# Moving the sums of inputs for the block products behind units of the second pass's first chunk

## Chip, cores and metric

One core of a Trainium2 chip runs the kernel. The metric is the device time of one execution in microseconds (us); lower is better. Several executions are timed and their median is given, and one more is recorded by the profiler.

## What is computed

Attention over 4 batches and 12 heads (448 positions, 64 wide) gives x of 1792 x 768. Two feed-forward layers follow, each with 2048 hidden columns:

```python
def _moe_ref(x, w_in, w_out, s, b):
    h = x @ w_in
    r = np.maximum(h, 0.0)
    g = s * (r * r) + b
    return g @ w_out

def _moe2_ref(x, w_in, w_out):
    h = x @ w_in
    g = h * np.cos(h)
    return g @ w_out

def reference(q, k, v, g_q, g_k, moe, moe2):
    x = attention(q, k, v, g_q, g_k).transpose(0, 2, 1, 3).reshape(1792, 768)
    return _moe2_ref(_moe_ref(x, **moe), **moe2)
```

All of it is fp32. The change touches the first layer alone, and in it only the input product `x @ w_in` of batches 2 and 3.

## The kernel before

**Products.** TensorE takes fp32 operands as two parts, a high one (a cast, made on ScalarE) and a low one (value minus high, a subtraction on VectorE or GpSimd). Each product is three matmuls: high by high, high by low, low by high. Weights are tiles wh, wl; inputs xha, xla; hidden values gh, gl. A matmul here has 128 rows of contraction, 128 rows out and 448 columns, one batch.

**Staging.** The hidden columns are cut into 8 chunks of two 128-row blocks. The list `segs` sets the order: segments 0 to 2 do layer 1 for batches 0 and 1 beside the attention, segment 3 does layer 1 for batches 2 and 3 (the second pass), segment 4 is layer 2. A chunk has input units (`unit_in`: 18 matmuls into a PSUM tile ph, then ScalarE's relu r, GpSimd's square r2, VectorE's scale and bias gt, ScalarE's cast gh and GpSimd's low part gl) and 12 output units per pair of batches (`unit_out_1`: 6 matmuls into a PSUM tile po, which on the first visit ScalarE copies to acc and later VectorE adds to acc).

**The second pass.** Its first chunk is done with four plain input units (two blocks for batch 2, then two for batch 3: 72 matmuls) and its 12 output units, the six of batch 2 ahead of the six of batch 3 (72 matmuls). From the second chunk on, `unit_seven` replaces the four input units of a chunk by seven block products of 9 matmuls (a11, s2, s3, s1, a12, a22, s4). They need sums of the weight blocks (`load_combined`: tiles rs, ts, cast to wsh and low part wsl) and sums of the input blocks t1 to t4. The input sums are made once, by `combine_x(c)` for c = 0, 1, 2: four DMAs bring blocks from DRAM into tiles xc, VectorE makes four differences in place (lines 624 to 627), ScalarE four casts into xhb (line 630), VectorE two and GpSimd two low parts into xlb (line 631). `unit_seven` sums its products in two tiles uh and ul (line 683 on VectorE, line 700 the copy of the first product on ScalarE), with one buffer each. Its PSUM tiles share three buffers of tag ph with `unit_in`; po has three buffers too.

**Where the pools meet.** At `("next", 3)` the attention's pools are closed and the pools xb, mb and psb are opened. The PSUM banks of psb were those of other tiles until then, and the first ph of the second pass has to wait for the last adds to acc of the segment before. The tiles xc share one ring of 8 buffers (tag "acc" in mb) with the weight sums wsh and wsl of `load_combined`: xc of c = 2 takes the places of c = 0, and the weight sums of chunk 1 take the places of c = 1.

**Order.** The program runs under a scheduling context that decides the order of instructions on each engine; each engine then runs its own list in order. Two helpers bind it: `follow` adds a real wait, `issue_after` only an order. The dictionary `marks` holds instructions that later ones are put behind.

The call before the change, in the main loop over units:

```python
                pools["psb"] = ctx.enter_context(tc.tile_pool(name="psb", bufs=2, space=PSUM))
                for c in range(NE // 2):
                    combine_x(c)
            continue
```

Of the kernel before, what the change touches and what calls it, by code (L numbers as in the profile page):

```python
# [10 lines left out]
F32 = mybir.dt.float32  # L11
# [4 lines left out]
ALU = mybir.AluOpType  # L16
# [27 lines left out]
def body(ctx, tc, q, k, v, g_q, g_k, w1_in, w1_out, s_in, b_in, w2_in, w2_out, out):  # L44
    nc = tc.nc
    B, H, S, D = q.shape
    E = out.shape[1]
    F = w1_in.shape[1]
    P = 128
# [6 lines left out]
    NE = E // P  # L56
# [5 lines left out]
    NT = 2 * S // P  # L62
# [19 lines left out]
    pools = {"att": att_scope.enter_context(tc.tile_pool(name="att", bufs=2))}  # L82
# [6 lines left out]
    sb = const.tile([P, 2], F32, tag="sb", name="sb")  # L89
# [10 lines left out]
    marks = {}  # L100
# [5 lines left out]
    def issue_after(later, earlier):  # L106
        info = mybir.DependencyInfo(mybir.DependencyClass.NoSync, mybir.DependencyReason.DATA)
        tc.add_manual_dep(later.ins, earlier.ins.name, info, reason="issue order")
# [9 lines left out]
    def home(layer, b):  # L118
        return held_x["b" if layer and b < 2 else "a"]
# [10 lines left out]
    def wide(layer, seg, ck):  # L130
        return layer == 1 or seg == 3 and 0 < ck < NCK - 1

    def span(layer, seg, ck, b):
        cut = WIDE if wide(layer, seg, ck) else S
        return slice(cut, 2 * S) if b % 2 else slice(0, cut)

    def products(w, x):
        return ((w[0], x[0]), (w[1], x[0]), (w[0], x[1]))
# [478 lines left out]

    mixed = {}

    def combine_x(c):  # L620
        x11, x12, x21, x22 = (pools["mb"].tile([P, E], F32, tag="acc", name=f"xc_{c}_{n}", bufs=2 * NT - NE)[:, :S] for n in range(4))
        for t, b, cc in ((x11, 2, c), (x12, 3, c), (x22, 3, c + NE // 2), (x21, 2, c + NE // 2)):
            nc.sync.dma_start(t, stash[0, b, cc])
        nc.vector.tensor_tensor(x11, x12, x11, ALU.subtract)
        nc.vector.tensor_tensor(x12, x22, x12, ALU.subtract)
        nc.vector.tensor_tensor(x22, x22, x11, ALU.subtract)
        nc.vector.tensor_tensor(x21, x21, x22, ALU.subtract)
        for n, (name, t) in enumerate((("t1", x11), ("t3", x12), ("t2", x22), ("t4", x21))):
            hi, lo = mixed[name, c] = [z[:, n // 2 * S:(n // 2 + 1) * S] for z in held_x["b"][c + n % 2 * (NE // 2)]]
            nc.scalar.copy(hi, t)  # L630
            (nc.vector if n % 2 else nc.gpsimd).tensor_tensor(lo, t, hi.bitcast(F32), ALU.subtract)  # L631

    g = {}
    acc = {}
# [3 lines left out]
    def g_pair(key, seg):  # L638
        n = count["pairs"] % (5 if seg > 3 else 4)
        count["pairs"] += 1  # L640
        if "mb" not in pools or n < 3:
            gp, tag, nb = ma, "g", 3
        else:
            gp, tag, nb = pools["mb"], "gx"[n - 3], 1
        return [gp.tile([P, 2 * S], F32R, tag=tag + z, name=f"g{z}_{key}", bufs=nb) for z in "hl"]

    def squared(h, key, place=None):
        def temp(pool, tag, name):
            return pool.tile([P, WIDE], F32, tag=tag, name=f"{name}_{key}")[:, :h.shape[1]]

        r = temp(ma, "t0", "r") if place is None else place
        nc.scalar.activation(r, h, AF.Relu)
        r2 = temp(pools["mb"], "t1", "r2") if "mb" in pools else r
        nc.gpsimd.tensor_tensor(r2, r, r, ALU.mult)
        gt = temp(ma, "t2", "gt")
        nc.vector.tensor_scalar(gt, r2, sb[:, 0:1], sb[:, 1:2], ALU.mult, ALU.add)
        return gt

    def unit_seven(layer, seg, ck, *_):
# [55 lines left out]
    def unit_in(layer, seg, ck, f, b):  # L715
        ft = ck * CF + f
        key = f"{layer}_{ft}_{b}"
        wh, wl = weights[layer, seg, 0, ft, 0]
        wh, wl = (z.rearrange("p (c f) -> p c f", f=P) for z in (wh, wl))
        pool, tag, bufs = (pools["psb"], "ph", 3) if "psb" in pools else (psm, "mo", 2)  # L720
        ph = pool.tile([P, 512], F32, tag=tag, name=f"ph_{key}", bufs=bufs)
        at = span(layer, seg, ck, b)
        size = at.stop - at.start
        h = ph[:, :size]

        def temp(pool, tag, name):
            return pool.tile([P, WIDE], F32, tag=tag, name=f"{name}_{key}")[:, :size]

        for c in range(NE):
            x = [z[:, at] for z in home(layer, b)[c]]  # L730
            for n, (a, m) in enumerate(products((wh[:, c, :], wl[:, c, :]), x)):
                nc.tensor.matmul(h, a, m, start=(c == 0 and n == 0), stop=(c == NE - 1 and n == 2))  # L732
            if c % 2 and c < NE - 1:
                yield 1.13
        if count["g"] % 2 == 0:
            pair[:] = g_pair(key, seg)
        to = at if wide(layer, seg, ck) else slice(count["g"] % 2 * S, (count["g"] % 2 + 1) * S)
        gh, gl = (z[:, to] for z in pair)
        count["g"] += 1
        if layer == 0:  # L740
            gt = squared(h, key)
        else:
            hs = temp(ma, "t0", "hs")
            marks["hs"] = nc.scalar.copy(hs, h)
            h = hs
            kk = temp(pools["mb"], "t1", "kk")
            nc.scalar.activation(kk, h, AF.Copy, scale=1.0 / (2 * math.pi), bias=MAGIC)
            nc.scalar.activation(kk, kk, AF.Copy, bias=-MAGIC)  # L748
            gt = temp(ma, "t2", "gt")
            nc.vector.scalar_tensor_tensor(gt, kk, -C1, h, ALU.mult, ALU.add)  # L750
            nc.vector.scalar_tensor_tensor(gt, kk, -C2, gt, ALU.mult, ALU.add)
            nc.scalar.activation(gt, gt, AF.Abs)
            nc.scalar.activation(gt, gt, AF.Sin, scale=-1.0, bias=halfpi)  # L753
            nc.gpsimd.tensor_tensor(gt, h, gt, ALU.mult)  # L754
        nc.scalar.copy(gh, gt)  # L755
        nc.gpsimd.tensor_tensor(gl, gt, gh.bitcast(F32), ALU.subtract)  # L756
        g[ft, b] = (gh, gl)
        if layer == 1 and b % 2:
            g[ft, "pair", b // 2] = list(pair)
        yield 1.13  # L760
# [173 lines left out]
    def ahead(n):  # L934
        while todo and todo[0][0] - AHEAD * (todo[0][1][0] == "s") <= n:
            count["needed"], key = todo.pop(0)
            if key[0] == "s":
                load_combined(key[1])
            else:
                load_weight(key)  # L940
# [3 lines left out]
    def until(batches):  # L944
        while finished["pairs"] < batches * NP:
            next(steps)
# [9 lines left out]
    debt = 0.0  # L956
    seg = 0
    soon, again = [], []
    wait = 0
    for n, u in enumerate(units):  # L960
        count["unit"] = n
        ahead(n + LOOK)
        if u[0] == "next":
            seg = u[1]
            if seg == 1:
                until(2)
            if seg == 3:
                for _ in steps:
                    pass
                att_scope.close()  # L970
                pools["xb"] = ctx.enter_context(tc.tile_pool(name="xb", bufs=1))
                held_x["b"] = paired(pools["xb"], "b")
                pools["mb"] = ctx.enter_context(tc.tile_pool(name="mb", bufs=2))
                pools["psb"] = ctx.enter_context(tc.tile_pool(name="psb", bufs=2, space=PSUM))
                for c in range(NE // 2):
                    combine_x(c)
            continue
        if wait:
            wait -= 1
        elif soon:  # L980
            reload(*soon.pop(0))
        elif again:
            reload(*again.pop(0))
        if u[0] == "in":
            while soon and len(xs.get((u[1], u[5]), [])) < NE:
                reload(*soon.pop(0))
            while again and u[1] == 1:
                reload(*again.pop(0))
        for cost in {"in": unit_in, "seven": unit_seven, "out": unit_out}[u[0]](*u[1:]):
            debt += cost * rates[min(seg, 1)]  # L990
            while debt > 0:
                c = next(steps, None)
                if c is None:
                    break
                debt -= c
        if u[0] == "seven" and u[3] == NCK - 1:
            again = [(1, b, c) for b in range(2) for c in range(NE)]
        if n in last:
            until(last[n] + 1)
            if finished["pairs"] == B * NP:  # L1000
                fetch(last[n])
                wait = 3
            soon += [(0, last[n], c) for c in range(NP)]
# [28 lines left out]
```

## Time and profile before

| | |
|---|---|
| median of 3 executions | 1250.6 us (1248.45 to 1252.15) |
| the profiled execution | 1251.13 us, span 1249.3 us |
| busy share of the span | PE 98%, PE weight loads 83%, DVE 72%, ACT 62%, POOL 52% |
| mean granted TensorE clock | 0.996 |
| chain that ended last | PE 79%, DVE 4%, POOL 2%, DMA 2%, ACT 2% |
| longest waits of PE | 6.6 us (one, first ph of the second pass), 4.0 us in 3, 2.9 us in 2 |

PE is TensorE, PEld its weight loads, DVE is VectorE, ACT ScalarE, POOL GpSimd, SP SyncE (it issues the DMAs). Times in rows are microseconds from the start of the span unless they say ns. A bracket behind a row of a timeline gives the idle time of the engine just before it and what ended that. Since PE is busy for 98% of the span, time on the other engines counts where PE waits for them.

### The profile page before, as it was taken

Reading aid. Unit: us, or ns where it says so; the run is one execution under the profiler, and the core shown is the slowest. Engines: PE = TensorE matmul, PEld = TensorE weight load, DVE = VectorE, ACT = ScalarE, POOL = GpSimd, SP = SyncE. Lnnn points to the kernel's source line nnn. Section 1 sums busy time; section 2 is a strip of 40 time slices with the busy share of each in tenths; the row PEclk is TensorE's granted clock in tenths of the full one; section 3 lists DMA queues with packets and bytes.
Section 4 is the critical chain, followed back from the end, with each engine's and each line's share of the span. In section 5 each row is a group of like instructions: output and inputs, shape, how many; then the busy total and the mean of one; then the engine's idle time right before and its main releaser. Section 6 shows DMA issues by size and latency. Waiting matters only on the chain.

```text
span 1249.3 us, 18909 instructions
## 1 busy us (share of the span) xinstructions
PE 1219.8 (98%) x6566; PEld 1033.2 (83%) x6566; DVE 894.0 (72%) x1514; ACT 768.8 (62%) x1705; POOL 648.7 (52%) x758
## 2 busy tenths in 40 slices
PE   7999999999999999979999999999999999999998
PEld 5555777778777877978899889899999999999997
DVE  6888778777768764785877788575777766676765
ACT  4788888776657653545334346698666766565640
POOL 4777647464544534765554544556454535353541
PEclk9999999999999999989999999999999999999999
DMA  4334336334333433451222241131111111111105
GB/s 120 98 104 121 105 99 193 113 131 141 107 123 97 128 112 122 159 176 46 76 58 64 72 144 43 35 109 57 51 51 51 51 51 51 51 51 52 55 9 177
DMA packets 88462, 114.07 MB, mean 91 GB/s; under 512 B 11952, under 2 KB 78512, under 8 KB 88368
## 3 DMA queue, kind: packets, MB, share of 16 engines
q1 hardware_dynamic: 88048, 112.66, 29.6%
q8 instruction: 51, 0.84, 0.3%
q14 instruction: 43, 0.35, 0.1%
q10 hardware_dynamic: 320, 0.23, 0.1%
HBM read 89.26 MB, written 23.59 MB: 90 GB/s over the span
## 4 chain that ended last, share of the span: by engine, by line
PE 79%; DVE 4%; POOL 2%; DMA 2%; ACT 2%; issue 1%; SPq 0%; DVEq 0%; ACTq 0%; POOLq 0%
PE ph L732 27%; PE po L810 18%; PE po L784 15%; PE av L406 4%; PE tp L371 4%; PE sc L319 4%; PE ph_s L676 3%; PE ph_a L676 2%; DMA t<-wd 1%; POOL xlb L631 1%; DVE wl L537 1%; PE rt L390 1%; DMA rs<-wd 0%; PE pt_q L276 0%; POOL wsl L603 0%
## 5 line engine op out<-in xcount | busy, mean ns | idle before, releaser
L537 POOL TENSOR_TENSOR wl<-t,wh 128x384 fp32r<-128x384 f32 x128 | 140.5, 1114 | 88.6 <-ACT wh L534 82.0
L756 POOL TENSOR_TENSOR gl<-gt,gh 128x512 fp32r<-128x512 f32 (+1 forms) x100 | 120.2, 1213 | 114.7 <-ACT gh L755 114.5
L732 PE MATMUL ph<-xha,wh 128*128 128x448 f32 (+2 forms) x408 | 152.1, 373 | 6.8 <-DVE acc L792 6.6
L810 PE MATMUL po<-wh,gh 128*128 128x384 f32 x448 | 152.0, 340 | 1.3 <-DVE acc L818 1.3
L818 DVE TENSOR_TENSOR acc<-po,acc 128x384 f32<-128x384 f32 x196 | 105.3, 551 | 64.2 <-PE po L810 63.9
L732 PE MATMUL ph<-xha,wl 128*128 128x448 f32 (+2 forms) x408 | 150.3, 368 | 0.0
L810 PE MATMUL po<-wh,gl 128*128 128x384 f32 x448 | 150.1, 335 | 0.0
L810 PE MATMUL po<-wl,gh 128*128 128x384 f32 x448 | 149.5, 335 | 0.0
L732 PE MATMUL ph<-xla,wh 128*128 128x448 f32 (+2 forms) x408 | 149.5, 368 | 0.0
L754 POOL TENSOR_TENSOR gt<-hs,gt 128x512 f32<-128x512 f32 x64 | 76.7, 1205 | 117.1 <-ACT gt L753 113.3
L792 DVE TENSOR_TENSOR acc<-po,acc 128x448 f32<-128x448 f32 (+2 forms) x168 | 101.5, 617 | 45.2 <-PE po L784 44.4
L578 DVE SCALAR_TENSOR_TENSOR t<-c,t 128x384 uint32<-128x384 uint32 x128 | 97.6, 765 | 40.2 <-ACT t L572 36.8
L534 ACT CAST wh<-t 128x384 fp32r<-128x384 f32 x172 | 82.5, 511 | 62.6 <-PE po L784 20.0
L346 ACT ACTIVATE pr<-sc,top 128x448 f32<-128x448 f32 x161 | 102.2, 640 | 17.2 <-DVE top L334 16.6
L334 DVE TENSOR_REDUCE top<-sc 128x1 f32<-128x448 f32 x168 | 98.2, 615 | 16.2 <-PE sc L319 15.4
L571 ACT ACTIVATE c<-raw 128x384 f32<-128x384 f32 x128 | 71.2, 558 | 52.4 <-DVE t L579 16.4
L371 PE MATMUL tp<-ident,pr 128*112 128x128 f32 x672 | 94.9, 278 | 1.6 <-ACT pT L385 0.7
L371 PEld LDWEIGHTS tp<-ident,pr 128*112 128x112 f32 x672 | 74.5, 134 | 25.5 <-issue 13.3
L732 PEld LDWEIGHTS ph<-xha,wh 128*128 128x128 f32 x408 | 77.3, 189 | 17.4 <-ACT xhb L630 6.9
L810 PEld LDWEIGHTS po<-wh,gh 128*128 128x128 f32 x448 | 84.0, 188 | 8.9 <-DVE acc L818 6.1
L579 DVE SCALAR_TENSOR_TENSOR t<-c,t 128x384 uint32<-128x384 uint32 x128 | 88.3, 693 | 1.8
L750 DVE SCALAR_TENSOR_TENSOR gt<-kk,hs 128x512 f32<-128x512 f32 x64 | 55.5, 869 | 47.2 <-ACT kk L748 26.6
(182 smaller groups left out, 3232.5 us busy)
## 6 DMA issues: line engine op xcount, KB each, us to landing
raw<-in_moe_w_in_dram SPq DMA_DIRECT2D x64, 384.0 KB, 3.5
raw<-in_moe_w_out_dram SPq DMA_DIRECT2D x64, 384.0 KB, 3.2
wd<-t SPq DMA_DIRECT2D x64, 192.0 KB, 2.6
t<-wd SPq DMA_DIRECT2D x44, 192.0 KB, 2.4
rawk<-in_k_dram SPq DMA_DIRECT2D x24, 224.0 KB, 2.8
rawv<-in_v_dram SPq DMA_DIRECT2D x24, 224.0 KB, 3.0
rs<-wd SPq DMA_DIRECT2D x28, 192.0 KB, 2.6
rawq<-in_q_dram SPq DMA_DIRECT2D x23, 192.0 KB, 2.8
```

The lines of the kernel that those rows point to most:

```text
L334: line("DVE", nc.vector.tensor_reduce(top, st[i]["sc", c][j][1][:, :S], axis=AX.X, op=ALU.max, negate=True))
L346: e = line("ACT", nc.scalar.activation(pr, sc[:, :S], AF.Exp, bias=st[i]["top"][:, at], scale=scale, accum_out=st[i]["sums"][:, at]))
L371: mm = [nc.tensor.transpose(tp[:, kc * P:(kc + 1) * P], pr[:, kc * CP:(kc + 1) * CP], ident) for kc in range(NCH)]
L537: casts.append((count["needed"], z, eng, eng.tensor_tensor(wl, w, wh.bitcast(F32), ALU.subtract)))
L578: nc.vector.scalar_tensor_tensor(t, c, 0x80000000, t, ALU.bitwise_and, ALU.bitwise_or)
L579: nc.vector.scalar_tensor_tensor(t, c, 3, t, ALU.logical_shift_left, ALU.bitwise_or)
L732: nc.tensor.matmul(h, a, m, start=(c == 0 and n == 0), stop=(c == NE - 1 and n == 2))
L756: nc.gpsimd.tensor_tensor(gl, gt, gh.bitcast(F32), ALU.subtract)
L784: marks["out"] = nc.tensor.matmul(po, a, m, start=(f == 0 and n == 0), stop=(f == CF - 1 and n == 2))
L792: nc.vector.tensor_tensor(at, po, at, ALU.add)
L810: nc.tensor.matmul(po, a, m, start=(f == 0 and n == 0), stop=(f == CF - 1 and n == 2))
L818: nc.vector.tensor_tensor(at, po, at, ALU.add)
```

## The change

`combine_x` is cut in two: `fetch_x(c)` issues the four DMAs, `combine_x(c)` the arithmetic. At `("next", 3)` only `fetch_x(0)` and `fetch_x(1)` are called. The arithmetic is called in the loop over units, behind the third, fourth and sixth place after it: c = 0 behind the second input unit, c = 1 behind the third, c = 2 behind the first output unit; `fetch_x(2)` stands directly behind `combine_x(0)`. The first difference of each c is put behind the latest gt on VectorE, and each cast xhb behind the latest gh on ScalarE. No instruction is added or taken away; every engine has as many rows as before. Lines from 624 on stand 3 lines lower after the change (624 is 627, 631 is 634, 656 is 659, 732 is 735), those from 756 on in `unit_out_1` as well (790 is 793, 792 is 795).

```diff
-    def combine_x(c):
-        x11, x12, x21, x22 = (pools["mb"].tile([P, E], F32, tag="acc", name=f"xc_{c}_{n}", bufs=2 * NT - NE)[:, :S] for n in range(4))
+    def fetch_x(c):
+        x11, x12, x21, x22 = mixed["raw", c] = [pools["mb"].tile([P, E], F32, tag="acc", name=f"xc_{c}_{n}", bufs=2 * NT - NE)[:, :S] for n in range(4)]
         for t, b, cc in ((x11, 2, c), (x12, 3, c), (x22, 3, c + NE // 2), (x21, 2, c + NE // 2)):
             nc.sync.dma_start(t, stash[0, b, cc])
-        nc.vector.tensor_tensor(x11, x12, x11, ALU.subtract)
+
+    def combine_x(c):
+        x11, x12, x21, x22 = mixed.pop(("raw", c))
+        issue_after(nc.vector.tensor_tensor(x11, x12, x11, ALU.subtract), marks["gt"])
...
-            nc.scalar.copy(hi, t)
+            issue_after(nc.scalar.copy(hi, t), marks["gh"])
...
-        nc.vector.tensor_scalar(gt, r2, sb[:, 0:1], sb[:, 1:2], ALU.mult, ALU.add)
+        marks["gt"] = nc.vector.tensor_scalar(gt, r2, sb[:, 0:1], sb[:, 1:2], ALU.mult, ALU.add)
...
-        nc.scalar.copy(gh, gt)
+        marks["gh"] = nc.scalar.copy(gh, gt)
...
-                for c in range(NE // 2):
-                    combine_x(c)
+                for c in range(2):
+                    fetch_x(c)
+                sums = {n + 2: (0,), n + 3: (1,), n + 5: (2,)}
...
+        for c in sums.get(n, ()):
+            combine_x(c)
+            if c == 0:
+                fetch_x(2)
```

**First place: VectorE, the last adds to acc of the segment before, ahead of the second pass's first matmul.** The adds are those of line 792 (795 after); wl_3_0_1_0 is the low part of the second block of the first chunk's weights. Before:

```order
L624 TENSOR_TENSOR xc_0_6679<-xc_1_6680,xc_0_6679 128x448
L631 TENSOR_TENSOR xlb_6648<-xc_1_6660,xhb_6647 128x448
L537 TENSOR_TENSOR wl_3_0_1_0_6543<-t_3_0_1_0_0_6544,wh_3_0_1_0_6542 128x384
L627 TENSOR_TENSOR xc_2_6661<-xc_2_6661,xc_3_6662 128x448
L792 TENSOR_TENSOR acc_0_3_0_2425<-po_0_3_1_6596,acc_0_3_0_2425 128x448
L537 TENSOR_TENSOR wl_3_0_1_0_6543<-t_3_0_1_0_1_6548,wh_3_0_1_0_6542 128x384
L625 TENSOR_TENSOR xc_1_6680<-xc_3_6682,xc_1_6680 128x448
L792 TENSOR_TENSOR acc_0_4_0_2482<-po_0_4_1_6606,acc_0_4_0_2482 128x448
L792 TENSOR_TENSOR acc_0_5_0_2519<-po_0_5_1_6616,acc_0_5_0_2519 128x448
```

After:

```order
L537 TENSOR_TENSOR wl_3_0_1_0_6543<-t_3_0_1_0_0_6544,wh_3_0_1_0_6542 128x384
L795 TENSOR_TENSOR acc_0_3_0_2425<-po_0_3_1_6596,acc_0_3_0_2425 128x448
L537 TENSOR_TENSOR wl_3_0_1_0_6543<-t_3_0_1_0_1_6548,wh_3_0_1_0_6542 128x384
L795 TENSOR_TENSOR acc_0_4_0_2482<-po_0_4_1_6606,acc_0_4_0_2482 128x448
L795 TENSOR_TENSOR acc_0_5_0_2519<-po_0_5_1_6616,acc_0_5_0_2519 128x448
```

The differences xc and the low part xlb are gone from between the adds; the two halves of wl_3_0_1_0 still stand ahead of the last two adds.

**Second place: VectorE, from the end of the first chunk's input units to the first weight sum of chunk 1.** wsl_0 is the low part of the product a11's weights. Before, with no gt of batch 2 or 3 ahead of these rows:

```order
L631 TENSOR_TENSOR xlb_6648<-xc_2_6661,xhb_6647 128x448
L626 TENSOR_TENSOR xc_3_6682<-xc_3_6682,xc_0_6679 128x448
L631 TENSOR_TENSOR xlb_6650<-xc_1_6680,xhb_6649 128x448
L624 TENSOR_TENSOR xc_0_6699<-xc_1_6700,xc_0_6699 128x448
L537 TENSOR_TENSOR wl_3_1_0_0_6587<-t_3_1_0_0_1_6592,wh_3_1_0_0_6586 128x384
L627 TENSOR_TENSOR xc_2_6681<-xc_2_6681,xc_3_6682 128x448
```

After:

```order
L659 TENSOR_SCALAR gt_1_3_6885<-r_0_1_3_6883,sb 128x448
L627 TENSOR_TENSOR xc_0_6743<-xc_1_6744,xc_0_6743 128x448
L628 TENSOR_TENSOR xc_1_6668<-xc_3_6670,xc_1_6668 128x448
L628 TENSOR_TENSOR xc_1_6744<-xc_3_6746,xc_1_6744 128x448
L629 TENSOR_TENSOR xc_3_6670<-xc_3_6670,xc_0_6667 128x448
L629 TENSOR_TENSOR xc_3_6746<-xc_3_6746,xc_0_6743 128x448
L630 TENSOR_TENSOR xc_2_6669<-xc_2_6669,xc_3_6670 128x448
L634 TENSOR_TENSOR xlb_6650<-xc_1_6668,xhb_6649 128x448
L630 TENSOR_TENSOR xc_2_6745<-xc_2_6745,xc_3_6746 128x448
L634 TENSOR_TENSOR xlb_6652<-xc_1_6744,xhb_6651 128x448
L603 TENSOR_TENSOR wsl_0_6761<-rs_0_6751,wsh_0_6760 128x384
```

The sums of c = 1 and c = 2 now stand behind the last gt of the first chunk (gt_1_3) and ahead of the weight sum that chunk 1's first product needs.

**Third place: GpSimd, the same stretch.** gl_0_3 are the low parts of the hidden values of batch 3, xlb_6644 and xlb_6646 the sums' low parts. Before:

```order
L631 TENSOR_TENSOR xlb_6644<-xc_0_6679,xhb_6643 128x448
L631 TENSOR_TENSOR xlb_6644<-xc_3_6682,xhb_6643 128x448
L631 TENSOR_TENSOR xlb_6646<-xc_0_6699,xhb_6645 128x448
L654 TENSOR_TENSOR r_0_0_2_6742<-r_0_2_6740 128x448
L603 TENSOR_TENSOR wsl_1_6787<-ts_0_6781,wsh_1_6786 128x384
```

After:

```order
L657 TENSOR_TENSOR r_0_1_3_6883<-r_1_3_6881 128x448
L759 TENSOR_TENSOR gl_0_3_6806<-gt_0_3_6811,gh_0_3_6805 128x448
L634 TENSOR_TENSOR xlb_6644<-xc_0_6667,xhb_6643 128x448
L759 TENSOR_TENSOR gl_0_3_6806<-gt_1_3_6885,gh_0_3_6805 128x448
L634 TENSOR_TENSOR xlb_6646<-xc_0_6743,xhb_6645 128x448
L634 TENSOR_TENSOR xlb_6644<-xc_3_6670,xhb_6643 128x448
L603 TENSOR_TENSOR wsl_0_6761<-ts_1_6758,wsh_0_6760 128x384
```

The low parts xlb stood ahead of the first square r of batch 2; they now stand behind the last square of batch 3, mixed with the low parts gl that the output units read.

## Rows read from the trace of the kernel before

**Rows 1.** Page: busy time of each engine and share of the span.

```profile
PE 1219.8 (98%) x6566; PEld 1033.2 (83%) x6566; DVE 894.0 (72%) x1514; ACT 768.8 (62%) x1705; POOL 648.7 (52%) x758
```

**Rows 2.** Waits of PE: line and releaser; us in total, times, longest.

```profile
PE ph L732 <- DVE acc L792: 6.6, 1, 6.6
```

**Rows 3.** PE timeline, early and around the first ph: start, us, operation, idle before.

```profile
16.21 1.63 PE L319 MATMUL sc<-kT,qT 64*128 64x448 f32 x4 [2.87 <-ACT pr L346]
...
536.80 0.37 PE L784 MATMUL po<-gl,wh 128*128 128x448 f32 x1
543.75 0.71 PE L732 MATMUL ph<-xha,wh 128*128 128x448 f32 x1 [6.58 <-DVE acc L792]
...
545.00 0.57 PE L732 MATMUL ph<-xha,wh 128*128 128x448 f32 x1
545.38 0.57 PE L732 MATMUL ph<-xha,wl 128*128 128x448 f32 x1
...
549.45 0.37 PE L732 MATMUL ph<-xha,wl 128*128 128x448 f32 x1
549.66 0.36 PE L732 MATMUL ph<-xla,wh 128*128 128x448 f32 x1
```

**Rows 4.** DVE timeline, 541 to 551.

```profile
541.04 0.95 DVE L537 TENSOR_TENSOR wl<-t,wh 128x384 fp32r<-128x384 f32 x1
...
542.46 1.14 DVE L792 TENSOR_TENSOR acc<-po,acc 128x448 f32<-128x448 f32 x2
...
550.15 0.61 DVE L631 TENSOR_TENSOR xlb<-xc,xhb 128x448 fp32r<-128x448 f32 x1
550.69 0.61 DVE L627 TENSOR_TENSOR xc<-xc,xc 128x448 f32<-128x448 f32 x1
```

**Rows 5.** ACT timeline, 537 to 553.

```profile
537.89 0.51 ACT L534 CAST wh<-t 128x384 fp32r<-128x384 f32 x1 [1.78 <-DMA t<-wd]
...
547.25 0.57 ACT L630 CAST xhb<-xc 128x448 fp32r<-128x448 f32 x1 [0.44 <-DVE xc L627]
...
552.77 0.54 ACT L652 ACTIVATE r<-ph 128x448 f32<-128x448 f32 x1
```

**Rows 6.** Windows: stretch, length, busy PE, PEld, DVE, ACT, POOL, then PEclk, DMA share, GB/s.

```profile
17.00:18.00 1.00, 1.00 (x5) 0.23 (x2) 0.40 (x2) 0.82 (x4) 0.26 (x1) 0.50 0.64 199
...
544.00:546.00 2.00, 2.00 (x6) 1.78 (x7) 2.00 (x5) 0.83 (x2) 0.19 (x1) 0.50 0.98 323
```

**Rows 7.** POOL timeline, 545 to 559 and 586 to 595.

```profile
545.81 7.62 POOL L631 TENSOR_TENSOR xlb<-xc,xhb 128x448 fp32r<-128x448 f32 x2 [4.23 <-ACT xhb L630]
...
555.26 1.30 POOL L631 TENSOR_TENSOR xlb<-xc,xhb 128x448 fp32r<-128x448 f32 x1
556.53 1.33 POOL L603 TENSOR_TENSOR wsl<-rs,wsh 128x384 fp32r<-128x384 f32 x1
557.82 1.47 POOL L756 TENSOR_TENSOR gl<-gt,gh 128x448 fp32r<-128x448 f32 x1
...
586.38 1.16 POOL L695 TENSOR_TENSOR gl_s<-gt_s,gh_s 128x448 fp32r<-128x448 f32 x1 [2.53 <-ACT gh_s L694]
...
593.65 1.08 POOL L654 TENSOR_TENSOR r_s<-uh 128x448 f32<-128x448 f32 x1
```

**Rows 8.** DVE timeline, 555 to 560.

```profile
555.48 2.80 DVE L603 TENSOR_TENSOR wsl<-rs,wsh 128x384 fp32r<-128x384 f32 x2
558.19 1.57 DVE L631 TENSOR_TENSOR xlb<-xc,xhb 128x448 fp32r<-128x448 f32 x1
```

**Rows 9.** ACT timeline, where chunk 2's first product is copied.

```profile
594.76 0.53 ACT L700 COPY uh<-ph_a 128x448 f32<-128x448 f32 x1 [0.22 <-POOL r_s L654]
```

**Rows 10.** PE timeline, 553 to 600: the rows with idle before them.

```profile
577.55 0.47 PE L784 MATMUL po<-gh,wh 128*128 128x448 f32 x1 [0.57 <-ACT acc L790]
...
595.35 0.47 PE L676 MATMUL ph_s<-xhb,wsh 128*128 128x448 f32 x1 [0.23 <-ACT uh L700]
...
598.07 0.51 PE L784 MATMUL po<-gh_s,wh 128*128 128x512 f32 x1 [0.63 <-ACT gh_s L694]
```

More of the change, by code (lines that the diff above doesn't have):

```diff
@@ L958, in body @@
     soon, again = [], []
+    sums = {}
     wait = 0
```

## The prediction, made before the changed kernel was run

> **What bounds the kernel now.** The page comes first: TensorE is busy for 98% of the span [rows 1], so an edit on the other engines counts only where TensorE waits, or where its clock is low. The list of its waits shows where: one wait of 6.6 us stands out, the first ph of the second pass behind the last adds to acc [rows 2]. The timeline of TensorE shows it: the last po begins at 536.80, the first ph at 543.75 after 6.58 us of idle [rows 3]. Behind the gap the matmuls come 0.375 us apart, later 0.203 [rows 3]. [...] From 543.75 to the end of the wide spacing at 548.7 there are some 14 matmuls, each late by 0.17, so the low clock costs 2.4 us. The timelines of VectorE and ScalarE say what the gap is made of: differences of xc stand between the adds, the last two adds run at 542.46 [rows 4], and a half of a weight cast waits for its DMA until 537.89 [rows 5].
>
> **Term 1, the gap closes in part.** The cast at 537.89 and its DMA [rows 5] stay where they are: on SP nothing ahead of that DMA moves, and the four DMAs of c = 2 only go further back. In the new order VectorE's wl of that cast still stands ahead of the last two adds. So: cast done at 538.4, wl 0.55, two adds 1.14 [rows 4], and 0.15 to the matmul as now (543.60 to 543.75), which is 540.2. TensorE idles 3.0 us instead of 6.58: **-3.6**. The bounds are 0 (if something else were to hold the bank) and -4.1 (if the wl were free earlier); the chain above is made of rows only, so I take its value.
>
> **Term 2, the clock.** The nearest row to a 3.0 us gap is the one of 2.87 us at 16.21, and there the clock fell as well, to 0.50 [rows 3, 6]; but TensorE was only partly busy before it, while here it comes from full work. So the clock may stay up at this gap (-2.4) or not (0). The terms below give two more gaps of about 3 us, each of which can bring it down. I count one low stretch, as now: **0**, with -2.4 and +2.4 (two stretches) kept as ends.
>
> **Term 3, the sums now fall into the first chunk's own work.** What hid them was the gap and the 72 matmuls of the input units, in which GpSimd had little else to do. From 540.2, the 72 matmuls take 14.6 us (0.203 each [rows 3]), to 554.8; the 42 output matmuls of batch 2 and of the first of batch 3 would end at 563.3, and then the first product of chunk 1 wants its weight sum. Behind the last ph come r (0.54 [rows 5]), its square (1.0) and gt (0.5), at 557.0. Then VectorE has ten operations up to that weight sum, 0.54 each [rows 4], 5.3 us, and GpSimd five (two gl, three xlb; one xlb pair also holds the ring places that the weight sum needs), 1.14 each as in undisturbed rows [rows 7], 5.7 us. If the two run side by side the weight sum's cast and low part (1.0) end at 563.7: 0.4 us of wait. If they exclude one another it is 557.0 + 11.0 + 1.0 = 569.0: 5.7 us. The rows speak for exclusion: two xlb on GpSimd, 2.3 us of work, took 7.62 us while VectorE ran differences and low parts back to back up to 551.3 [rows 4, 7]; and from 555.26 to 559.76 three operations of GpSimd and three of VectorE, 4.8 us of work by their undisturbed durations, took 4.5 us [rows 7, 8]. So I take 5.7, and 0.9 more because the sums and their casts are handed between VectorE and ScalarE (two waits of 0.44 in the trace, one of them in [rows 5]), now with copies of po between them on ScalarE: **+6.6**, between 0.4 and 9. It will show in pieces: at the later po of batch 2, whose three banks wait for ScalarE's copies, at the first po of batch 3 (low part gl on GpSimd), and at ph of product a11.
>
> [...]
>
> **Term 4, chunk 1 runs without cover.** Before, output matmuls of the first chunk stood between the products of chunk 1. Now most are spent earlier, and s1, a12, a22, s4 and chunk 2's a11, s2, s3 follow one another directly. Chunk 2's s1 is the fourth user of three PSUM banks and needs the copy of a11 into uh, which waits for the last square r_s of chunk 1 [rows 9]. From the end of chunk 1's s1, TensorE has six products to do, 54 x 0.203 = 11.0 us. GpSimd has seven operations up to that square, 1.05 each in the rows, 7.4 us, with 1.8 ahead (add and relu) and 0.6 behind (the copy): 9.8, no wait. With operations stretched by VectorE as at 555.26 to 557.82 (1.3 to 1.47 instead of about 1.1 [rows 7]) it is 12 to 13, a wait of 1 to 2; with the four waits for casts that these seven rows had before, the longest 2.53 and 4.6 in all [rows 7], a wait of 3.4 to 4.6. I take **+3.3**, with 0 and 6 as ends, since the casts and gt still stand in the same rows.
>
> **Term 5.** The three small waits of the trace at 577.55, 595.35 and 598.07 lie in the stretch that is now ordered otherwise [rows 10]; terms 3 and 4 take their place: **-1.4**.
>
> **Sum.** -3.6 + 0 + 6.6 + 3.3 - 1.4 = **+4.9**. Beyond 600 TensorE has next to no idle time, so the shift stays to the end. The sum is made against the profiled execution, 1251.1, which stands 0.5 above the median; against the median it is 1250.6 + 4.9 = **1255.5**.
>
> **Rivals.**
> - *The forecast*, both port-bound waits appear and the clock has one low stretch: 1253 to 1258. Chance 0.45.
> - *The sums slip in between (the other side).* If GpSimd's five operations and VectorE's ten overlap by more than about two thirds, term 3 is 2 or less and term 4 is 0 to 1: -3.6 + 1.5 + 0.5 - 1.4 = -3.0 with a low stretch, -5.4 without one: 1245 to 1248. For it: GpSimd has no run of more than five such operations, and VectorE's timeline has gaps in which they could go. Against it: the two overlaps above. Chance 0.15.
> - *Gain and loss cancel.* Term 3 about 4, term 4 about 1.5, clock up: -3.6 - 2.4 + 4 + 1.5 - 1.4 = -1.9; with the low stretch +0.5: 1248.5 to 1252. For it: these terms are bounded by 0.4 and 0 below. Chance 0.25.
> - *The clock falls twice*, at the first gap and at one of the later ones: +2.4, 1258 to 1260. Chance 0.10.
> - *The change doesn't do what it says*, because the first ph waits for something other than the adds: term 1 is 0, the rest as above or less, 1254 to 1259. The releaser named is the add, which speaks against it. Chance 0.05.
>
> **How the numbers follow.** About 0.3%, 3.75 us, is what can be told from no change. Faster than 1246.85 is two thirds of the second case and a little of the third: 0.13. Within: the rest of the second, nearly all of the third, a third of the forecast: 0.40. Slower than 1254.35: two thirds of the forecast and the last two cases: 0.47. The range from 1247 to 1259.5 leaves out about a tenth below and less above. The likeliest sign's own range is 1253 to 1258.
>
> **What would show it right or wrong.** The wait of the first ph falls to about 3.0 us and its matmul starts near 540.2 (right), or stays over 5 (term 1 wrong). New waits of PE between 558 and 572, on ScalarE's copies of po, on gl and on the weight sum, 6 to 7 us in all; GpSimd's xlb and gl of several us beside VectorE's run (term 3). One wait of 3 us or more of a product of chunk 2 on the copy into uh (term 4). The windows' granted clock at the gaps (term 2). If the new waits add up to under 4 us, the forecast falls and the kernel is level or faster.

## The result: slower by 0.8%, as forecast in sign and twice as much in size

The changed kernel takes 1259.86 us (median of 4, 1258.54 to 1261.97), the kernel before 1250.46 beside it: a ratio of 1.0077, 95% interval 1.0056 to 1.0098. The forecast was 1255.5, with a range up to 1259.5. So the sign was right, the size was not: +9.4 us where +4.9 was forecast, and the measured time lies just above the range.

The page of the changed kernel, its span, its engines (compare [rows 1]) and the clock in 40 slices:

```profile
span 1260.2 us, 18915 instructions
...
PE 1224.3 (97%) x6566; PEld 1035.3 (82%) x6566; DVE 902.2 (72%) x1514; ACT 769.7 (61%) x1705; POOL 647.2 (51%) x758
...
PEclk9999999999999999998999999999999999999999
```

The same line of the clock before:

```profile
PEclk9999999999999999989999999999999999999999
```

TensorE does the same matmuls and is busy for 4.5 us longer, and the mean granted clock of the profiled execution has fallen from 0.996 to 0.991. That is the first hint that idle time is not the whole loss. The slices are too coarse to show it: one slice stands below 9 in both kernels. The waits of TensorE from 530 to 640, which answer to [rows 2] (line and releaser; us in total, times, longest):

```profile
PE ph_s L679 <- ACT uh L703: 4.1, 1, 4.1
PE ph_a L679 <- DVE wsl L603: 3.3, 1, 3.3
PE ph L735 <- DVE acc L795: 3.3, 1, 3.3
```

The one wait of 6.6 us is now 3.3, and new ones of its size follow; two smaller groups are left out here. The timeline of TensorE shows where; it answers to [rows 3] and [rows 10]:

```profile
536.96 0.37 PE L787 MATMUL po<-gl,wh 128*128 128x448 f32 x1
540.61 0.44 PE L735 MATMUL ph<-xha,wh 128*128 128x448 f32 x1 [3.28 <-DVE acc L795]
...
563.54 0.47 PE L787 MATMUL po<-gh,wh 128*128 128x448 f32 x1 [1.67 <-ACT acc L793]
565.43 0.74 PE L787 MATMUL po<-gh,wh 128*128 128x448 f32 x1 [0.41 <-ACT acc L793]
568.41 0.74 PE L787 MATMUL po<-gh,wh 128*128 128x448 f32 x1 [0.36 <-ACT acc L793]
574.70 0.48 PE L679 MATMUL ph_a<-xha,wsl 128*128 128x448 f32 x1 [3.31 <-DVE wsl L603]
600.17 0.44 PE L679 MATMUL ph_s<-xhb,wsh 128*128 128x448 f32 x1 [1.33 <-ACT gh_s L697]
606.33 0.74 PE L679 MATMUL ph_s<-xhb,wsh 128*128 128x448 f32 x1 [4.06 <-ACT uh L703]
```

And the windows show the clock there (stretch, length, busy us of PE, PEld, DVE, ACT, POOL, then granted clock, DMA share, GB/s; compare [rows 6]):

```profile
542.00:544.00 2.00, 2.00 (x7) 1.74 (x6) 1.28 (x3) 0.51 (x1) 0.00 (x0) 0.50 0.90 314
...
566.00:568.00 2.00, 2.00 (x6) 1.30 (x4) 2.00 (x2) 1.07 (x3) 2.00 (x2) 0.50 0.00 0
...
576.00:578.00 2.00, 2.00 (x6) 1.76 (x6) 1.33 (x1) 0.49 (x2) 0.85 (x1) 0.50 0.00 0
...
607.00:609.00 2.00, 2.00 (x7) 1.78 (x6) 1.50 (x3) 0.56 (x1) 1.07 (x2) 0.50 0.35 100
```

Four stretches at a granted clock of 0.50 instead of 1.00, 541 to 544.7, 565 to 572, 575.4 to 578.8 and 606 to 609.5, where the kernel before has one.

**The account closes.** A late row marks the whole shift, the first input product of layer 2 that waits for ScalarE. Before and after:

```profile
798.71 0.44 PE L732 MATMUL ph<-xha,wh 128*128 128x384 f32 x1 [0.27 <-ACT hs L744]
809.56 0.44 PE L735 MATMUL ph<-xha,wh 128*128 128x384 f32 x1 [0.27 <-ACT hs L747]
```

With the 0.16 us that separated the runs already at 536.8 taken off, the shift is 10.7 us. Idle time of TensorE between the two marks: before 6.58 + 0.57 + 0.23 + 0.63 and one of 0.92 at 612.1, together 8.9; after the seven above and one of 0.24 at 762.6, together 14.7. That is +5.7. Clock: TensorE is busy at a granted clock of 0.50 for 5.2 us before and some 15.6 us after; matmuls come 0.375 us apart there instead of 0.203, so 0.46 of each such us is lost, 2.4 before and 7.2 after. That is +4.8. Together 10.5 of 10.7. (The profiled execution is the slowest of the four; the median shifts by 9.4.)

### The profile page after: what moved, and what is told of

Same layout as the page of the kernel before. It is cut to its first block, busy times and chain, and to the rows that moved or that the text cites. A ratio compares the mean times of both kernels' runs of the same rounds, so it can differ in the third digit from the quotient of the medians.

```text
span 1260.2 us, 18915 instructions
## 1 busy us (share of the span) xinstructions
PE 1224.3 (97%) x6566; PEld 1035.3 (82%) x6566; DVE 902.2 (72%) x1514; ACT 769.7 (61%) x1705; POOL 647.2 (51%) x758
## 4 chain that ended last, share of the span: by engine, by line
PE 80%; DVE 5%; issue 1%; POOL 1%; DMA 1%; ACT 1%; SPq 0%; DVEq 0%; ACTq 0%; POOLq 0%
PE ph L735 27%; PE po L813 18%; PE po L787 16%; PE av L406 4%; PE tp L371 4%; PE sc L319 4%; PE ph_s L679 3%; PE ph_a L679 2%; DMA t<-wd 1%; PE rt L390 1%; DVE wl L537 1%; PE pt_q L276 0%; DVE acc L795 0%; PE pt_k L276 0%; POOL wl L537 0%
## 5 line engine op out<-in xcount | busy, mean ns | idle before, releaser
L334 DVE TENSOR_REDUCE top<-sc 128x1 f32<-128x448 f32 x168 | 98.2, 615 | 16.4 <-PE sc L319 15.6
```

Source lines behind the costliest of these rows:

```text
L334: line("DVE", nc.vector.tensor_reduce(top, st[i]["sc", c][j][1][:, :S], axis=AX.X, op=ALU.max, negate=True))
```

## The experiments

Theory: the sums, put behind the first chunk's units, hold up GpSimd and VectorE, which take turns there (one operation of each per 1.53 us), and through them TensorE; behind the waits of 3.28, 3.31 and 4.06 us the granted clock was 0.50 as well. Rivals: the ring of tiles or the later DMAs; each engine's own queue; a clock that only takes the place of waiting.

**1. The split without the order.**

```diff
-        issue_after(nc.vector.tensor_tensor(x11, x12, x11, ALU.subtract), marks["gt"])
+        nc.vector.tensor_tensor(x11, x12, x11, ALU.subtract)
...
-            issue_after(nc.scalar.copy(hi, t), marks["gh"])
+            nc.scalar.copy(hi, t)
```

> The changed kernel without its two order marks: the DMAs are still issued apart and the sums are still called in the loop, but nothing binds them behind gt or gh. The scheduler then puts the differences back between the adds to acc, as before. Theory (the new place of the sums on VectorE and GpSimd makes all of the loss): the first ph waits 6.6 us again, one low stretch of the clock, no wait on a weight sum or on uh over 1 us, 1250.5 within 2. Rival (the later DMAs of c = 2 and the shared ring make part of the loss): 1253 or more, with waits on DMAs of xc or on ring places.

Measured: 1251.72, ratio 1.0006 (0.9997 to 1.0015), the first ph waits 7.5 us again, no other wait over 1 us. The split of the DMAs costs nothing that can be told; the scheduler puts the sums back into the gap. All of the loss comes from the order on VectorE. (The mark on ScalarE's casts adds nothing to it: without that mark alone the program has the same instructions in the same order on every engine as the changed kernel.)

**2. Sums behind the adds only.**

```diff
-        nc.vector.tensor_tensor(at, po, at, ALU.add)
+        marks["add"] = nc.vector.tensor_tensor(at, po, at, ALU.add)
...
-        nc.vector.tensor_tensor(x11, x12, x11, ALU.subtract)
+        issue_after(nc.vector.tensor_tensor(x11, x12, x11, ALU.subtract), marks["add"])
```

> The kernel before, with one edit: the first difference of each c is put behind the last add to acc, so the sums leave the gap but run in the stretch of the 72 input matmuls and not behind it. Theory (closing the gap alone is worth about 3.3 us, and the sums cost what they hold up on GpSimd): first ph waits 3.0 to 3.3, then waits of 3 to 7 us in all at the output matmuls of batch 2, because GpSimd's squares and low parts gl stand behind the sums; 1248 to 1254. Rival (the sums have free cover under the 72 matmuls): 1246 or less with no wait over 1 us behind the first.

Measured: 1249.93, ratio 0.9998 (0.9988 to 1.0007). Its waits of TensorE:

```profile
PE ph_s L676 <- ACT wsh L602: 3.6, 1, 3.6
PE ph L732 <- DVE acc L792: 3.1, 1, 3.1
```

The gap closes as far as in the changed kernel, and 3.6 us come back, though not where I expected them: not at the output matmuls, but at chunk 1's second product, behind the weight sum. TensorE idles less than before up to layer 2 (7.5 us against 8.9), but the granted clock falls to 0.50 twice, at 540 and at 567 (mean of the profiled execution 0.995, before 0.996). Closing the gap is worth about what the displaced work then costs. What loses time is therefore not that the sums left the gap, but how far they went.

**3. Low parts on VectorE.**

```diff
-            (nc.vector if n % 2 else nc.gpsimd).tensor_tensor(lo, t, hi.bitcast(F32), ALU.subtract)
+            nc.vector.tensor_tensor(lo, t, hi.bitcast(F32), ALU.subtract)
```

> The changed kernel with all twelve low parts xlb on VectorE (0.54 us each there, 1.14 on GpSimd), none on GpSimd. Theory (VectorE's two-input operations and GpSimd's exclude one another, so their sum counts): the sum of work in the stretch falls by some 3 us, the waits of term 3 from 5.75 to 2 to 4, the wait on uh stays at 4 or more; 1257 to 1259. Rival (each engine's own queue is the bound): VectorE, with more to do, comes later to the weight sum, the waits grow by 1.5 or more; 1261 or more.

Measured: 1256.22, ratio 1.0046 (1.0031 to 1.0061). VectorE has six operations more, and TensorE waits 11.6 us from 530 to 640 instead of 14.4. Its three longest groups:

```profile
PE ph_s L679 <- ACT uh L703: 5.9, 1, 5.9
PE ph L735 <- DVE acc L795: 2.9, 1, 2.9
PE po L787 <- ACT acc L793: 1.5, 2, 0.8
```

The wait of 3.3 us on the weight sum is gone; the rest of term 3 is 1.5 us, less than the 2 to 4 expected, and the time is a little under the range given. The rival is out: a longer queue on VectorE made the weight sum come sooner. The trace of this run shows why: GpSimd has nothing to do from 564.5 to 566.7, and VectorE's operations there come 0.54 us apart, against 1.5 in the changed kernel. The wait on uh has grown from 4.1 to 5.9 us, and two of the four low stretches of the clock are gone: matmuls come 0.37 us apart from 540.9 to 543.2 and from 600.5 to 604.7, but 0.20 from 567.8 to 580.5.

**4. Fillers in the waits.** 50 matmuls whose results nobody reads, in the four places where TensorE waited:

```diff
+    def filler(n, behind):
+        pt = psm.tile([P, 512], F32, tag="mo", name=f"fill_{count['fill']}", bufs=2)[:, :S]
+        count["fill"] += 1
+        x = home(0, 2)[0][0]
+        for k in range(n):
+            z = nc.tensor.matmul(pt, x[:, :P], x[:, :S], start=True, stop=True)
...
+            if (ck, wn) == (1, "a11"):
+                last[:] = [filler(13, outs_of[0, 0, 3])]
+            if (ck, wn) == (2, "s1"):
+                last[:] = [filler(17, last[0])]
```

> The changed kernel with 50 more matmuls of 448 columns on TensorE (10.2 us at 0.203 each), whose results nobody reads, put into the four places where it waited: 13 ahead of the first ph, 7 ahead of the fifth po of batch 2, 13 ahead of product a11 of chunk 1, 17 ahead of product s1 of chunk 2. Nothing else waits for them. Theory (four stretches at the lower clock cost some 7 us, against 2.4 in the kernel before): the engine is busy through the waits, the granted clock stays at 1.00 behind them, the first product of each place starts when it did or up to 1 us later, and the time falls by 4 to 7 us, to 1253 to 1256. Rival (the low clock only takes the place of waiting for other engines): the time stays within 1.5 us of 1259.9 or grows by what the fillers overrun.

Measured: 1256.55, ratio 1.0047 (1.0031 to 1.0064), 3.3 us under the changed kernel by the medians; the two intervals overlap a little (1.0056 to 1.0064). The profiled executions differ by more, 1260.2 and 1254.9 of span. Windows of the run with fillers:

```profile
541.00:543.00 2.00, 2.00 (x11) 1.85 (x10) 0.68 (x2) 0.51 (x1) 0.00 (x0) 1.00 1.02 375
...
566.00:568.00 2.00, 1.61 (x4) 1.50 (x5) 2.00 (x4) 1.52 (x4) 0.84 (x2) 0.56 0.00 0
...
575.00:577.00 2.00, 2.00 (x12) 1.81 (x11) 1.31 (x3) 1.38 (x3) 0.94 (x1) 1.00 0.07 10
...
606.00:608.00 2.00, 2.00 (x12) 1.82 (x11) 2.00 (x4) 1.36 (x3) 1.56 (x2) 1.00 0.13 26
```

The first ph still begins at 540.13 (540.61 without fillers), since it waits for the same add; but the matmuls behind it run at a granted clock of 1.00. Only the stretch at 566 is still low (0.56); the fillers put there had ended ahead of a wait of 1.51 us. More work on TensorE made the kernel faster: the loss at the lower clock is real and not hidden behind other waits. The gain is smaller than expected, and the time lies 0.5 us above the range given.

**5. Squares of the seven products on ScalarE.**

```diff
-        nc.gpsimd.tensor_tensor(r2, r, r, ALU.mult)
+        if place is None:
+            nc.gpsimd.tensor_tensor(r2, r, r, ALU.mult)
+        else:
+            nc.scalar.activation(r2, r, AF.Square)
```

> The changed kernel with the squares behind the seven products (four a chunk) made by ScalarE instead of GpSimd. Theory (the wait of 4.1 us for the copy into uh is GpSimd's queue behind products that follow one another directly): that wait falls under 1 us and the low stretch of the clock behind it goes, 3.5 to 5.5 us less, 1254 to 1256.5; the waits before 575 stay. Rival (the wait comes from the products' own chain, or from VectorE's sums): it stays over 2.5 us, 1258 or more.

Measured: 1256.02, ratio 1.0046 (1.0031 to 1.0061). Its waits:

```profile
PE ph_a L682 <- DVE wsl L603: 4.3, 1, 4.3
PE po L790 <- ACT acc L796: 3.6, 3, 1.7
PE ph L738 <- DVE acc L798: 2.6, 1, 2.6
PE ph_s L682 <- ACT uh L706: 0.8, 1, 0.8
```

The wait on the copy into uh falls from 4.1 to 0.8, the one ahead of a11 grows from 3.3 to 4.3, the rest stay about as they were. Two things keep this run from showing that GpSimd's squares made the wait. First, the edit also changes ScalarE's order: the copy now stands ahead of the cast of ts, which stood ahead of it in the changed kernel (its rows are shown under term 4):

```profile
598.47 0.53 ACT L706 COPY uh<-ph_a 128x448 f32<-128x448 f32 x1
...
600.71 0.51 ACT L602 CAST wsh<-ts 128x384 fp32r<-128x384 f32 x1
```

Second, the gain is not that wait's alone. Idle time up to layer 2 falls by only 1.6 us, but of the four low stretches only the one at a11 is left (matmuls 0.37 us apart from 572.7 to 575.7). The edit touches nothing before chunk 1; yet at 541 the clock stays up behind a wait of 2.58 us (matmuls 0.20 us apart; 3.28 and 0.375 in the changed kernel), and at 565 behind waits of 1.66, 0.41 and 1.50 us (1.67, 0.41 and 0.36):

```profile
566.00:568.00 2.00, 1.92 (x7) 1.24 (x7) 2.00 (x4) 1.53 (x4) 0.89 (x1) 1.00 0.00 0
```

The time came out as expected, in part for reasons that the theory doesn't have.

**6. Free banks, on the kernel before.** The first chunk's input units take their PSUM tiles from the two banks of the pool psm, which nobody uses by then.

```diff
-        pool, tag, bufs = (pools["psb"], "ph", 3) if "psb" in pools else (psm, "mo", 2)
+        pool, tag, bufs = (pools["psb"], "ph", 3) if "psb" in pools and (seg, ck) != (3, 0) else (psm, "mo", 2)
```

> The kernel before, with one edit: the four plain input units of the second pass's first chunk take their PSUM tiles from the pool of two banks that the adds have left free, instead of the banks that the last adds to acc still read. The sums stay where they were. Theory (the wait is for the bank and nothing else, and what follows it is bounded by GpSimd's queue, which the sums fill): the 6.6 us wait goes, the clock stays up or falls for less, waits of 0.5 to 2.5 us come up at the second unit's weights and at the output matmuls, 3 to 7 us in all; 1244 to 1248. Rival (the sums' place decides everything, the gap costs nothing): 1249 to 1252.

Measured: 1249.08, ratio 0.9984 (0.9975 to 0.9994). The gap of 6.6 us is gone altogether, the bank was its cause. But only 0.16%, 1.6 us by the medians, are left of the gain: the wait did what the theory said, the time lies where the rival put it. The longest of the waits that take its place (the mean granted clock of the profiled execution is 0.997, against 0.996 before and 0.999 in experiment 7):

```profile
PE ph_s L676 <- ACT wsh L602: 3.4, 1, 3.4
PE ph_a L676 <- DVE uh L683: 1.3, 1, 1.3
```

**7. The gap closed and GpSimd relieved.** Experiment 6, and all squares of the second pass on ScalarE.

```diff
-        nc.gpsimd.tensor_tensor(r2, r, r, ALU.mult)
+        if seg_now[0] == 3:
+            nc.scalar.activation(r2, r, AF.Square)
+        else:
+            nc.gpsimd.tensor_tensor(r2, r, r, ALU.mult)
```

> The kernel before with the free banks for the first chunk's input units (as in the run on free banks) and with all squares of the second pass on ScalarE. Theory (after the gap is gone, GpSimd's queue beside VectorE's sums is the next bound): the wait at product s2 of chunk 1 (3.4 us there) falls under 2, and the time is 2 to 5 us under that run, 1244 to 1247. Rival (what is left is VectorE's own queue, behind the ring of weight tiles): s2 waits as long as it did, 1248.5 to 1250.

Measured: 1246.92, ratio 0.9973 (0.9961 to 0.9985), faster than both kernels. From 530 to 640 no wait is over 1.0 us, and the clock stays up: matmuls of 448 columns come 0.20 us apart throughout, and the mean granted clock of the profiled execution is 0.999. The longest:

```profile
PE po L788 <- DVE acc L796: 1.0, 1, 1.0
PE po L788 <- POOL gl L760: 1.0, 1, 1.0
```

**8. The squares alone, on the kernel before** (the edit of 7 without that of 6).

> The kernel before with one edit: all squares of the second pass on ScalarE instead of GpSimd; banks and sums as before. Theory (with the sums in the gap, GpSimd's queue has slack; the bound is the gap): the first ph waits 6 to 7.5 us as before, the small waits up to 615 shrink, 1247.5 to 1250.5; so most of the 3.5 us of the run with free banks and squares on ScalarE needs both edits. Rival (the squares alone are the gain): 1246.5 to 1247.5.

Measured: 1248.13, ratio 0.9984 (0.9975 to 0.9993). The first ph still waits 5.7 us. Each edit alone gives 0.16%, both together 0.27%: the two gains about add up, and that most of the gain needs both edits is not borne out.

**9. The edits of 6 and 7 on the changed kernel.**

> The changed kernel with free banks for the first chunk's input units and all squares of the second pass on ScalarE: the two edits that brought the kernel before to 1246.9, put on the change. Theory (the changed place of the sums costs what it holds up on GpSimd and through that on ScalarE's copies; with 4 + 4 x 7 squares taken off GpSimd about half of it is left, ahead of a11): waits of 3 to 6 us between 555 and 575, one or two low stretches of the clock, 1247 to 1251, slower than the same two edits with the sums in the old place. Rival (only GpSimd's squares made the loss): 1246.9 or less.

Measured: 1249.55, ratio 0.9989 (0.9979 to 0.9999). It is 2.6 us behind experiment 7 by the medians, whose only difference is the place of the sums; the two intervals overlap a little (0.9979 to 0.9985). With no gap left to close and fewer squares on GpSimd, the new place still makes the weight sum late:

```profile
PE ph_a L683 <- DVE wsl L604: 5.1, 1, 5.1
PE po L791 <- ACT acc L797: 2.0, 1, 2.0
```

The two add up to 7.0 us, a little over the 3 to 6 expected; the time lies in the range given.

**10. Another mending of the change: free banks, low parts on VectorE, the seven products' squares on VectorE.** The squares' edit is shown; the other two are those of experiments 6 and 3. The mark on ScalarE's casts is left out too, which changes no engine's order here either.

```diff
-        nc.gpsimd.tensor_tensor(r2, r, r, ALU.mult)
+        (nc.gpsimd if place is None else nc.vector).tensor_tensor(r2, r, r, ALU.mult)
```

> The changed kernel with three edits: free banks for the first chunk's input units, all low parts xlb on VectorE, and the squares behind the seven products on VectorE. Theory (the sums' place is harmful only through GpSimd's queue and the clock that falls in the waits): no wait of 3 us or more is left, 1244 to 1248. Rival (the place itself is bad, since VectorE's sums stand ahead of the weight sums): waits of 3 us or more ahead of a11, 1250 or more.

Measured: 1255.42, ratio 1.0039 (1.0024 to 1.0054): a miss. With VectorE fuller, the output matmuls wait 3.8 us for a low part gl and 2.3 for a copy, and the clock falls behind both (matmuls 0.37 us apart from 569.7 to 572.7 and from 559.4 to 562.7):

```profile
PE po L787 <- POOL gl L759: 3.8, 1, 3.8
PE po L787 <- ACT acc L793: 2.3, 1, 2.3
```

How much of this is the place of the sums and how much the squares on VectorE is not shown, since the kernel before was not run with the same edits. Some of its loss also lies behind 640, where TensorE's waits add up to 5.1 us against 1.6 before. Why was not followed up.

## Why the prediction was right in sign and too small

**Term 1, right.** Forecast -3.6 by a start at 540.2; measured 3.28 of idle and a start at 540.61, so -3.3. The chain was the one read from the rows, wl, the two adds, the matmul behind them:

```profile
538.84 0.56 DVE L537 TENSOR_TENSOR wl<-t,wh 128x384 fp32r<-128x384 f32 x1 [3.33 <-ACT wh L534]
539.32 1.15 DVE L795 TENSOR_TENSOR acc<-po,acc 128x448 f32<-128x448 f32 x2
```

Experiment 6 shows that the bank was what it waited for.

**Term 2 is the step that failed.** "I count one low stretch, as now: 0, with -2.4 and +2.4 (two stretches) kept as ends." There were four, and term 2 measured +4.8. The row for it stood in [rows 3]: behind a wait of 2.87 us the granted clock had come down to 0.50 [rows 6]. The 2.4 itself comes from the spacing of the matmuls in [rows 3], in a stretch that [rows 6] gives a granted clock of 0.50. The prediction named three gaps of about 3 us in the changed kernel and then counted a fall for one. At its own price of 2.4 for a stretch, the three gaps that it named would have given +9.7, and a range that holds the result. Some of that nearness would have been luck: the fourth stretch, at 565, lies behind waits of 1.67 and 0.41 us that the prediction did not name, and the four cost less apiece, 1.5, 2.6, 1.5 and 1.5. Experiment 4 shows the loss directly.

**Term 3, right in mechanism and about right in size.** Forecast +6.6; measured 1.67 + 0.41 + 0.36 + 3.31 = 5.75, in the places named (banks of po behind ScalarE's copies, then the weight sum of a11), except that no separate wait on gl came up. What the prediction read as exclusion is plain in the timelines of the two engines, GpSimd first, then VectorE:

```profile
563.83 1.53 POOL L634 TENSOR_TENSOR xlb<-xc,xhb 128x448 fp32r<-128x448 f32 x1
565.32 1.53 POOL L759 TENSOR_TENSOR gl<-gt,gh 128x448 fp32r<-128x448 f32 x1
566.80 1.53 POOL L634 TENSOR_TENSOR xlb<-xc,xhb 128x448 fp32r<-128x448 f32 x1
```

```profile
564.27 3.05 DVE L628 TENSOR_TENSOR xc<-xc,xc 128x448 f32<-128x448 f32 x2
567.25 2.10 DVE L629 TENSOR_TENSOR xc<-xc,xc 128x448 f32<-128x448 f32 x2
...
569.80 1.56 DVE L634 TENSOR_TENSOR xlb<-xc,xhb 128x448 fp32r<-128x448 f32 x1
...
573.16 1.48 DVE L603 TENSOR_TENSOR wsl<-rs,wsh 128x384 fp32r<-128x384 f32 x1
```

Both engines go at one operation each per 1.5 us, the sum of 0.54 and about 1.0: they take turns. The 7.62 us of [rows 7], for 2.3 us of work, looked otherwise: there one engine was held up over a whole run of the other. For the sum both are the same, for what waits they are not. The forecast's first case calls the waits port-bound; no run shows a port, the runs show turns of 1.53 us. One piece of the working was off: the last gt of the first chunk was forecast to end at 557.0 and ended at 562.88, since it stood behind sums of c = 0 on VectorE, the late start and the low clock; the weight sum's chain behind it took 11.8 us, forecast 12.0. The output matmuls waited in that time too, so the wait did not grow with it.

**Term 4, right in place, too small by 2.1, and for the most part made by something else.** Forecast +3.3; measured 4.06 for the copy into uh and 1.33 for a bank in the same stretch, 5.4, inside the bounds given. The rows of GpSimd show the queue that the prediction counted; the last square of chunk 1 is the row at 601.47:

```profile
597.92 1.32 POOL L603 TENSOR_TENSOR wsl<-ts,wsh 128x384 fp32r<-128x384 f32 x1
600.17 1.34 POOL L698 TENSOR_TENSOR gl_s<-gt_s,gh_s 128x448 fp32r<-128x448 f32 x1 [0.93 <-ACT gh_s L697]
601.47 1.08 POOL L657 TENSOR_TENSOR r_s<-uh 128x448 f32<-128x448 f32 x1
```

GpSimd was nearly always busy, but the square ended at 602.55, 0.3 us after TensorE had fallen idle at 602.27. The copy came at 605.75, 3.2 us behind the square. Those 3.2 us are ScalarE's queue, in which a cast that waited for VectorE stood ahead of the copy:

```profile
605.33 0.51 ACT L602 CAST wsh<-ts 128x384 fp32r<-128x384 f32 x1 [2.56 <-DVE ts L607]
605.75 0.53 ACT L703 COPY uh<-ph_a 128x448 f32<-128x448 f32 x1
```

The prediction had counted GpSimd's operations and not what else stood ahead on ScalarE. Had the copy followed the square at once, the wait would have been about 0.9 us (an estimate from these rows: 0.3, the copy's 0.53 and the hand-overs). Experiment 5 took the squares off GpSimd and moved the copy ahead of that cast with one edit, so no run parts the two.

**Term 5.** Forecast -1.4, measured -2.3: a fourth small wait, 0.92 at 612.1, went as well.

**The rivals.** That the sums slip in between was given 0.15 and fell with the turn-taking above. That gain and loss cancel held for experiment 2, not for the change. That the clock falls twice was the rival that came nearest, with 0.10. Its times, 1258 to 1260, hold the result, but by luck: it counted two low stretches where there were four, shorter ones, and left term 4 at its forecast.

## What to carry to other kernels

Read every wait that a change would create twice: once for its length, once for whether the engine's clock may fall behind it, and let the range reach from no fall to one for every such wait. No length of a wait decided it in these traces: behind 2.87 us (the kernel before, granted clock 0.50) and 2.35 us (experiment 10, matmuls 0.37 us apart) the clock fell, behind 2.58 us (experiment 5, 0.20 apart) it did not. And work that fills a gap in the critical engine is well placed if it costs that gap less than it would cost elsewhere: here the sums in the gap were cheap, because nobody else wanted GpSimd then. When a gap has a cause of its own (a bank), remove the cause first, and move the work only if something is then late.

## What was not expected of the hardware

The granted clock fell to 0.50 behind single waits of 3.28, 3.31 and 4.06 us, but also at 565 in a stretch where the waits were only 1.67 and 0.41, and behind the first of them it fell only after TensorE was at work again: the matmuls at 540.89 and 541.09 were followed after 0.20 us, those from 541.29 on after 0.375. The wait had been over for 0.7 us when the clock fell. Nor do the same waits always cost it: in experiment 5 it stayed up at the first and second of these places, behind 2.58 us and behind 1.66, 0.41 and 1.50 us (matmuls 0.20 us apart). What makes it fall behind one wait and not behind a like one stays open here.

Useless matmuls in waits paid: 50 of them, 10.2 us of TensorE's time, made the changed kernel 3.3 us faster.
